# Where a retention-and-FFN kernel places its small side work: copies of turned q and k, and the preparation of w_out

## The chip, the cores and the metric

The kernel runs on one core of one Trainium2 chip. The metric is the device time of that core in microseconds (us), over repeated executions. A few terms are used throughout. PE is TensorE, PEld its weight loads, DVE is VectorE, ACT is ScalarE, POOL is GpSimd. PSUM holds PE's products; SBUF holds the other tiles on the chip. One execution of a kernel is profiled, and the span of the trace is about 1.7 us shorter than the time measured for that execution.

## The reference

```python
def _attn_ref(q, k, v):                       # q, k, v: 8 batches, 8 heads, 576 tokens, 64 wide
    scores = scale * np.matmul(q, k.transpose(0, 1, 3, 2))
    gamma = 1.0 - 2.0 ** (-5.0 - np.arange(H, dtype=np.float32))
    ...
    Dmat = np.where(rel >= 0, gamma[:, None, None] ** rel[None, :, :], 0.0)
    return np.matmul(scores * Dmat[None], v)

def _moe_ref(x, w_in, w_out):                 # x: 4608 x 512, w_in: 512 x 2048, w_out: 2048 x 512
    h = np.maximum(x @ w_in, 0.0)
    return (h * h @ w_out).astype(np.float32)

# reference: x = attention output, batch by batch, heads side by side; result = _moe_ref(x, ...)
```

Retention (attention without softmax, with a decay per head) makes the 4608 rows of x; a feed-forward layer with squared ReLU follows. Its two weight matrices are fed to the core as 64-bit numbers, and w_out has to be turned into 32-bit numbers on the core by bit operations before it can be used.

## The kernel before

The attention goes through the tokens in chunks of 128. Between the parts of a chunk's attention, the kernel runs **steps** of the first FFN product: a block is 512 tokens, and block n is done in 28 steps (n, mp, j), with mp from 0 to 3 and j from 0 to 6. The seven values of j are the seven products of a Strassen-like scheme, each four matmul calls in the code. Both matrices' sums for that scheme are done by DVE. The second FFN product, with w_out, begins only after the last attention chunk and the steps then left, at 583.5 us.

One chunk runs like this:

```python
            retain_a(i - 1)
            ...
            move(C, i)            # copies of turned q and k that chunk i needs now
            ffn(i - 1, 0)         # steps, "first half"
            retain_b(i - 1)       # q'U (turned q times the state U of earlier chunks), then a tiny ACT copy of two PSUM columns
            if i < N_CH:
                scores(i)
            retain_c(i - 1)       # the rest of the chunk; ACT copies x out of PSUM
            if N_TURN <= i + 2 < N_CH:
                flip(i + 2)       # queues two DVE transposes and 16 ACT copies
            ffn(i - 1, 1)         # steps, "second half"
```

The tiny copy matters because the matmuls of `retain_c` wait for it, and ACT takes its work in the order of issue.

```python
    def retain_b(i):
        ...                       # q'U on PE
        nc.scalar.copy(u_sb[(2 * ci + (cs // CH)) % 3][:, 0:2, 0:1], xp[0][:, :, cs - CH:cs - CH + 1])

    def retain_c(i):
        ...
        while at < tok + cs:
            n = at // TOK
            while steps and steps[0][0] <= n - 2:
                step()            # steps left over at a block's end
            end = min(tok + cs, (n + 1) * TOK)
            nc.scalar.copy(xT[n][...], p[...])        # frees the single x_ps tile
```

After its product, each step empties the product's PSUM buffer on ACT or DVE. A later product takes that buffer, so PE may have to wait for it:

```python
        elif j == 3:
            nc.scalar.activation(g["A11"], p, AF.Relu)                                # ACT, L638
            nc.gpsimd.tensor_tensor(g["A11"], g["A11"], g["A11"], op=ALU.mult)        # POOL, L639
        elif j == 4:
            nc.vector.tensor_tensor(g["A22"], p, p15, op=ALU.add)                     # DVE, L641
            square(g["A22"])                                                          # DVE, L629
```

Then each step may carry one **part** of the preparation of w_out, 139 parts in all. A piece of w_out is five DVE instructions and one pair on ACT; the outer sums follow after every second piece:

```python
    def w_out_parts():
        ...
            for one, two, beside, *_ in pair:
                yield one                 # DVE L210
                yield two, beside         # DVE L214, ACT L218 and L219: the conversion pair
            for i, (_, _, _, three, four, five) in zip((j - 1, j), pair):
                yield three               # DVE L222
                yield four                # DVE L225
                yield last                # DVE L228, and the fetch of a later piece
            ...
                r1, r2, r3, r4 = right_sums(*b)                # DVE L245 to L248
                yield lambda r1=r1, r2=r2: (r1(), r2())
                yield lambda r3=r3, r4=r4: (r3(), r4())
        ...
    # at the end of a step:
        if n_w2[0] < 0.9 * (done[0] - N_0):                                  # pace
            if not (busy[0] or held[0] and type(w_out_next[0]) is tuple):    # a tuple is L214 with its pair
                ...                                                          # issue the next part
```

## Time and profile before

| | before |
|---|---|
| time, median of 3 runs (range) | 985.23 us (984.21 to 985.42) |
| span of the trace | 981.6 us |
| PE busy, whole span | 954.2 us, 97% |
| first product of w_in in the steady part to last matmul of attention | 421.7 us |
| from there to the first product with w_out | 55.3 us |
| products with w_out | 398.1 us |

The three lower rows are read from the start times of PE's instructions. The change touches only the first of them. Two groups of instructions of the page before give the two engines that PE can be held up by there (line, engine, operation, tiles, shapes and count; then busy us and mean ns of one; then idle time before them and what ended most of it):

```profile
L622 PE MATMUL h_b<-room,w 128*128 128x256 f32 x768 | 186.6, 386 | 6.7 <-DVE room L641 3.7
L411 ACT COPY qk<-flip 32x256 f32<-32x256 f32 x416 | 167.4, 402 | 16.4 <-DVE flip L396 10.7
```

PE's products of one of three kinds lose 6.7 us to waits, 3.7 of them for L641. ACT's copies of turned q and k are 167.4 us of work in small instructions of 0.4 us: whatever comes after them in ACT's order has to sit through them. The waits themselves, and what lies ahead of them, are shown in the prediction.

### The profile page before, as it was taken

Reading aid. Unit: us, or ns where it says so; the run is one execution under the profiler, and the core shown is the slowest. Engines: PE = TensorE matmul, PEld = TensorE weight load, DVE = VectorE, ACT = ScalarE, POOL = GpSimd, SP = SyncE. Lnnn points to the kernel's source line nnn. Section 1 sums busy time; section 2 is a strip of 40 time slices with the busy share of each in tenths; the row PEclk is TensorE's granted clock in tenths of the full one; section 3 lists DMA queues with packets and bytes.
Section 4 is the critical chain, followed back from the end, with each engine's and each line's share of the span. In section 5 each row is a group of like instructions: output and inputs, shape, how many; then the busy total and the mean of one; then the engine's idle time right before and its main releaser. Section 6 shows DMA issues by size and latency. Waiting matters only on the chain. (4 is left out here: it accounts for less than half of the span.)

```text
span 981.6 us, 24018 instructions
## 1 busy us (share of the span) xinstructions
PE 954.2 (97%) x10108; PEld 850.8 (87%) x10108; DVE 781.8 (80%) x1447; ACT 341.6 (35%) x848; POOL 128.1 (13%) x121
## 2 busy tenths in 40 slices
PE   7799999999999989989999999999999999999998
PEld 6645787888878878878888889999999999999998
DVE  4789798978887988788756588878888787887876
ACT  3454384674755855846541010000000000000000
POOL 3221223312122221213201000000000000000000
PEclk9999999999999999999999999999999999999999
DMA  9975656785586767655636967645353454634241
GB/s 201 241 222 152 180 149 168 210 271 152 146 247 197 202 177 232 172 146 134 240 131 237 360 246 251 226 161 184 108 204 115 177 186 170 209 114 172 87 172 43
DMA packets 172011, 181.43 MB, mean 185 GB/s; under 512 B 118144, under 2 KB 132480, under 8 KB 165248
## 3 DMA queue, kind: packets, MB, share of 16 engines
q1 hardware_dynamic: 169792, 179.38, 57.9%
q8 instruction: 79, 1.29, 0.5%
q10 hardware_dynamic: 2112, 0.52, 0.2%
q14 instruction: 28, 0.23, 0.1%
HBM read 109.36 MB, written 70.52 MB: 183 GB/s over the span
## 5 line engine op out<-in xcount | busy, mean ns | idle before, releaser
L622 PE MATMUL h_b<-room,w 128*128 128x256 f32 x768 | 186.6, 386 | 6.7 <-DVE room L641 3.7
L411 ACT COPY qk<-flip 32x256 f32<-32x256 f32 x416 | 167.4, 402 | 16.4 <-DVE flip L396 10.7
L622 PEld LDWEIGHTS h_b<-room,w 128*128 128x128 f32 x768 | 144.0, 191 | 29.0 <-DVE room L641 4.9
L928 PE MATMUL o_b<-w,room 128*128 128x128 f32 x1168 | 144.4, 275 | 0.2 <-DVE room L880 0.2
L928 PEld LDWEIGHTS o_b<-w,room 128*128 128x128 f32 x1168 | 137.2, 192 | 0.4 <-DVE room L880 0.4
L928 PE MATMUL o_c<-w,room 128*128 128x128 f32 x1008 | 123.0, 275 | 0.0
L622 PE MATMUL h_a<-room,w 128*128 128x256 f32 x512 | 122.5, 382 | 0.0
L622 PE MATMUL h_c<-room,w 128*128 128x256 f32 x512 | 122.1, 381 | 0.0
L928 PEld LDWEIGHTS o_c<-w,room 128*128 128x128 f32 x1008 | 117.7, 192 | 0.0
L942 ACT COPY r<-o_a 128x128 f32<-128x128 f32 x53 | 14.1, 266 | 271.6 <-PE o_a L928 236.0
L622 PEld LDWEIGHTS h_a<-room,w 128*128 128x128 f32 x512 | 96.0, 190 | 13.9 <-issue 0.5
L622 PEld LDWEIGHTS h_c<-room,w 128*128 128x128 f32 x512 | 96.4, 190 | 13.4
L928 PE MATMUL o_a<-w,a 128*128 128x128 f32 x688 | 85.6, 275 | 0.0
L928 PEld LDWEIGHTS o_a<-w,a 128*128 128x128 f32 x688 | 81.2, 192 | 0.1
L639 POOL TENSOR_TENSOR room<-room 128x512 f32<-128x512 f32 x32 | 34.8, 1086 | 346.3 <-ACT room L638 291.8
L629 DVE SCALAR_TENSOR_TENSOR room<-room 128x512 f32<-128x512 f32 x96 | 71.5, 745 | 3.3
L586 PE MATMUL h_ps<-room,w 128*128 128x512 f32 (+1 forms) x152 | 58.9, 535 | 2.7 <-DVE w L228 1.8
L641 DVE TENSOR_TENSOR room<-h_b,room 128x512 f32<-128x512 f32 x32 | 22.0, 687 | 45.5 <-PE h_b L622 45.5
L376 POOL TENSOR_TENSOR q_ld<-q_ld,dv 128x512 f32<-128x512 f32 (+1 forms) x39 | 45.8, 1175 | 90.3 <-DMA q_ld<-in_q_dram 56.0
L465 PEld LDWEIGHTS x_ps<-qk,v_ld 64*64 64x64 f32 x1152 | 40.3, 136 | 19.4 <-issue 12.1
L465 PE MATMUL x_ps<-qk,v_ld 64*64 64x64 f32 x1152 | 49.6, 226 | 6.4 <-ACT u_sb L503 6.0
L453 POOL TENSOR_TENSOR v_ld<-v_ld,dv 128x512 f32<-128x512 f32 (+1 forms) x40 | 48.6, 1215 | 15.0 <-DMA v_ld<-in_v_dram 7.6
(104 smaller groups left out, 1339.8 us busy)
## 6 DMA issues: line engine op xcount, KB each, us to landing
g_dram<-room SPq DMA_DIRECT2D x32, 1280.0 KB, 5.7
a<-g_dram SPq DMA_DIRECT2D x30, 1024.0 KB, 6.1
room<-g_dram SPq DMA_DIRECT2D x15, 1024.0 KB, 5.6
w<-w_dram SPq DMA_DIRECT2D x7, 1792.0 KB, 9.8
out_dram<-room SPq DMA_DIRECT2D x17, 512.0 KB, 3.3
w<-in_moe_w_in_dram SPq DMA_DIRECT2D x16, 512.0 KB, 5.9
w<-in_moe_w_out_dram SPq DMA_DIRECT2D x16, 512.0 KB, 3.9
v_ld<-in_v_dram SPq DMA_DIRECT2D x31, 256.0 KB, 3.8
```

The costliest lines, as they stand in the source:

```text
L376: engine.tensor_tensor(t, t, dv[:cs, :, NCH + ci:NCH + ci + 1].to_broadcast([cs, H, D]), op=ALU.mult)
L411: nc.scalar.copy(*moves.pop(0)[2:])
L453: nc.gpsimd.tensor_tensor(vs[:cs], vs[:cs], dv[:cs, :, ci:ci + 1].to_broadcast([cs, H, D]), op=ALU.mult)
L465: own.append(lambda hp=hp, e=e, b=b: nc.tensor.matmul(x_at(hp, b, h), lhsT=s["vs"][rows(h), 2 * hp + b, :], rhs=s["ret"][rows(h), e, hp, : ...
L586: nc.tensor.matmul(p.rearrange("p h t -> p (h t)"), lhsT=w[:, c, :], rhs=xT[0][:, c, lo * HT:hi * HT], start=(c == 0), stop=(c == N_DM - 1))
L622: nc.tensor.matmul(p[:, mm, :], lhsT=w[:, c, :], rhs=xs[n][right][:, c, :], start=(j in OPENS and mm == 0 and c == 0), stop=(j in CLOSES a ...
L629: nc.vector.scalar_tensor_tensor(t, t, 0.0, t, op0=ALU.max, op1=ALU.mult)
L639: nc.gpsimd.tensor_tensor(g["A11"], g["A11"], g["A11"], op=ALU.mult)
L641: nc.vector.tensor_tensor(g["A22"], p, p15, op=ALU.add)
L928: nc.tensor.matmul(p, lhsT=s["lefts"][left][:, m, :], rhs=w_out[j][:, m, WO_SLOT[right], :], start=(i in OPENS and m == 0), stop=(i in CLO ...
L942: nc.scalar.copy(r[:, 0, 0:128], p)
```

## The change

Its intent is to keep three things out of the way of PE. Copies of turned q and k go two to a step, not three or four, in the half in front of q'U, and as before none in its last step, so that ACT is free when the tiny copy comes. No part of w_out goes into a step that carries a transpose, and no conversion pair into the last two steps of the first half. The outer sums of w_out go one to a step (155 parts in place of 139); to keep pace, steps j = 0 and 3 may take two parts, and the pace goes from 0.9 to 0.92 parts a step.

```diff
                 r1, r2, r3, r4 = right_sums(*b)
-                yield lambda r1=r1, r2=r2: (r1(), r2())
-                yield lambda r3=r3, r4=r4: (r3(), r4())
+                yield from (r1, r2, r3, r4)
@@ end of a step
-        if n_w2[0] < 0.9 * (done[0] - N_0):
-            if not (busy[0] or held[0] and type(w_out_next[0]) is tuple):
+        late_w2 = 0.92 * (done[0] - N_0) - n_w2[0]
+        for _ in range(0 if busy[0] else 2 if late_w2 > 1.5 and j in (0, 3) else late_w2 > 0):
+            if not (held[0] and type(w_out_next[0]) is tuple):
                 n_w2[0] += 1
                 f = w_out_next[0]
                 w_out_next[0] = next(w_out_steps, None)
                 for f in f if type(f) is tuple else (f,):
                     f and f()
-            if n == N_BLK - 2 and (mp, j) in ((2, 3), (3, 3)):
-                assert w_out_next[0] is None
-                fetch_w2(mp - 2)
+        if n == N_BLK - 2 and mp == 3 and j in (0, 3):
+            assert w_out_next[0] is None
+            fetch_w2(j // 3)
@@ in ffn
         while steps and count:
-            held[0] = half == 0 and count == 1
-            if not held[0]:
-                move(4 if len(moves) > 8 else 3)
-            busy[0] = len(flips) > 1
+            held[0] = half == 0 and count <= 2
+
+            move(4 if half and len(moves) > 8 else 3 if half else 2 if count > 1 else 0)
+            busy[0] = len(flips) > 0
```

## The prediction

> **What bounds the kernel now.** I read the page first, then busy time by stretch, then the waits of TensorE (PE) between 100 and 600 us, then ScalarE's (ACT) and VectorE's (DVE) instructions in order of time ahead of each wait, last the weight loads.
>
> Busy time in three stretches: the start; the stretch that the change touches; the w_out products. Columns: length, busy us (and count) of PE, PEld, DVE, ACT, POOL, then clock, DMA share, GB/s.
>
> ```profile
> 0.00:106.00 106.00, 94.84 (x1475) 61.36 (x1476) 79.29 (x131) 45.92 (x95) 26.10 (x31) 1.00 0.75 195
> 106.00:590.00 484.00, 471.29 (x5160) 401.54 (x5159) 388.21 (x610) 263.23 (x631) 102.02 (x90) 1.00 0.66 202
> 590.00:981.60 391.60, 388.10 (x3476) 387.91 (x3474) 314.31 (x708) 32.47 (x122) 0.00 (x0) 1.00 0.45 161
> ```
>
> PE is the bound throughout. Where the change works it stands idle 484.0 - 471.3 = 12.7 us. That is the whole purse, apart from slow clock and small gaps hidden in the modelled ends. The waits that make it up (total us, times, longest):
>
> ```profile
> PE x_ps L465 <- ACT u_sb L503: 5.5, 5, 1.5
> PE h_b L622 <- DVE room L641: 3.7, 3, 2.0
> PE h_b L622 <- DVE room L549: 2.2, 1, 2.2
> PE h_b L622 <- DVE room L634: 0.7, 2, 0.5
> ```
>
> Five times PE waits, after q'U and the scores, for a tiny ACT copy (0.16 us) that stands behind other ACT work; six times a product waits for DVE. Two examples. ACT ahead of a wait that ends at 253.78:
>
> ```profile
> 250.13 0.72 ACT L218 ACTIVATE w<-w,exp_bias 128x512 uint32<-128x512 uint32 x1
> 250.76 0.67 ACT L219 ACTIVATE w<-w 128x512 f32<-128x512 uint32 x1
> 251.46 1.65 ACT L411 COPY qk<-flip 32x256 f32<-32x256 f32 x4
> 253.13 0.60 ACT L638 ACTIVATE room<-h_a 128x512 f32<-128x512 f32 x1
> 253.62 0.16 ACT L503 COPY u_sb<-x_ps 128x2 f32<-128x2 f32 x1
> ```
>
> No line has idle time in front: ACT is simply late by two conversions of w_out and four copies. DVE ahead of the longest L641 wait, with POOL in the same time:
>
> ```profile
> 424.36 0.40 DVE L245 TENSOR_TENSOR w<-w 128x256 f32<-128x256 f32 x1
> 424.80 1.15 DVE L246 TENSOR_TENSOR w<-w 128x256 f32<-128x256 f32 x1
> 425.87 1.27 DVE L247 TENSOR_TENSOR w<-w,w 128x256 f32<-128x256 f32 x1
> 427.18 1.16 DVE L248 TENSOR_TENSOR w<-w,w 128x256 f32<-128x256 f32 x1
> 428.26 0.68 DVE L641 TENSOR_TENSOR room<-h_b,room 128x512 f32<-128x512 f32 x1
> ...
> 424.63 1.04 POOL L639 TENSOR_TENSOR room<-room 128x512 f32<-128x512 f32 x1 [10.59 <-ACT room L638]
> 425.63 1.24 POOL L376 TENSOR_TENSOR q_ld<-q_ld,dv 128x512 f32<-128x512 f32 x1
> 426.83 1.24 POOL L453 TENSOR_TENSOR v_ld<-v_ld,dv 128x512 f32<-128x512 f32 x1
> ```
>
> All four outer sums of w_out fall in two steps, in the 3.4 us in which POOL does its three products, and three of them take 1.2 us in place of 0.4. The clock after that wait:
>
> ```profile
> 423.30:429.00 5.70, 3.71 (x17) 2.95 (x17) 5.59 (x8) 3.49 (x9) 3.44 (x3) 1.00 1.09 298
> 429.00:432.60 3.60, 3.60 (x12) 2.41 (x12) 2.63 (x5) 1.28 (x2) 0.00 (x0) 0.53 0.42 83
> ```
>
> For 3.6 us the clock is 0.53, so the wait costs about 1.7 us more than its length.
>
> **What the Trainium skill says.** "TensorE: Matmul & The Clock Gate", section "What's actually happening": the clock is halved after an idle activity window of about 3.4 us, and the windows run freely. The trace agrees (0.53 over 3.6 us), though a 2.2 us wait at 293.8 did not halve it. The same page, "Architectural detail", has ACT and DVE as strict FIFO and PE as reordering weight loads only; both examples show it. "SBUF — State Buffer", section "Who interferes with whom": a DVE instruction with two SBUF inputs contends with a GpSimd one that reads SBUF. The four sums above show 0.40 us free, 1.15 to 1.27 us beside POOL. "Perfetto Trace Analysis", section "Identifying the Most-Contended Engine", warns that matmul busy time is no measure of nearness to roofline; so I count gaps in the stream, not busy share.
>
> **The change part by part.** It removes no work: PE's and POOL's instruction order is identical, DVE has the same instructions in another order, ACT too (but for how runs of copies fold). Only places move.
> (1) In the half in front of q'U, copies of turned q and k go two to a step rather than three or four, and none in the last step (as before).
> (2) In the last two steps there, not the last one, no conversion pair (L218 and L219, 0.72 + 0.67 = 1.4 us of ACT).
> (3) A step with either transpose gets no w_out part; before, the second one's step did.
> (4) Outer sums one to a step: 155 parts in place of 139. To keep pace, two parts go into steps j = 0 and 3 when they are behind. The last part falls late in block 7, near 523 us, not at its first steps; the first reload of w_out goes four steps later, but is needed only at 589 us, some 60 us on.
>
> I followed each wait into the new order. "Worth" is its length in PE's stream against the usual spacing, which exceeds the idle time shown where weight loads wait too.
> - 127.96 (1.3): ACT had 8 copies, a pair, 4 copies ahead. Now 8 and 2: 1.4 + 0.8 = 2.2 us less. Gone, -1.3.
> - 159.50 (1.65): a pair was held up by DVE right in front of the copy. The pair moves away. -1.65.
> - 253.92 (1.65): about 15 copies and two pairs become 10 copies and one pair. The ReLU of j = 3 still stands in front, so a little may stay. -1.5.
> - 347.04 (1.2): a pair and two copies less, 2.2 us. -1.2.
> - 527.53 (0.4): nothing queued ahead. Unchanged.
> - 151.49 (0.4): L228, 1.55 us beside POOL, leaves. -0.4.
> - 237.42 and 423.29 (0.35 and 0.6): DVE comes from the burst at a block's start (x's sums, two transposes); w_out work there is equal to 0.3 us. Unchanged.
> - 293.79 (2.3, behind x's sum L549): one sum of 0.55 us leaves; the part beside POOL (1.41) is replaced by another. -0.5.
> - 367.63 (1.7): L228 and one of four outer sums leave, but three still lie beside POOL. -0.8.
> - 429.00 (2.15 plus 1.7 of clock): L228 and four sums (4.6 us) become two wider sums, 1.2 to 2.8 us. L641 then ends by 427, in time. -3.85.
> Sum: -1.3 - 1.65 - 1.5 - 1.2 - 0.4 - 0.5 - 0.8 - 3.85 = -11.2 us.
>
> What it adds: in chunk 14 (64 rows, one step in its first half, near 187 us) two pairs now fall in the two steps ahead of that one. ACT then has a ReLU, a pair, four copies, a pair in front of the copy: 0.6 + 1.4 + 1.65 + 1.4, the second pair behind DVE's L641 and L629. I estimate 0.8 us of new wait. For other new ones I allow 0.8 us: DVE is busy 388 of 484 us, and doubled parts at j = 3 run into POOL's three products, which start when the ReLU of j = 3 ends. Net -11.2 + 1.6 = -9.6 us: 985.2 - 9.6 = 975.6 us.
>
> **The rivals.** (a) The waits only move. For: DVE's work is the same, and two parts at j = 3 sit at the worst place for POOL. Against: the waits come where DVE is late from a block's first step, and the change thins just those; the w_out work spreads over 12% more parts and steps. This gives 980 to 986. (b) All waits but the last go, and nothing new comes: -15 us, 970. Against: the bursts at 237, 293 and 423 are hardly touched. (c) Copies held back pile up, and scores wait for turned q and k: up to 8 are forced out in front of a first half (before, 8 at most too, but less often 8). That is 3.3 us of ACT against three steps of 1.73 us; I expect no wait. (d) DMA sets the end: stage buffers are written out and refilled, with six steps (10 us) between in the tightest place against transfers of about 10 us. If one is late, DVE blocks, and a stall of 2 us or more comes with slow clock: 978 to 982.
>
> **Range and chances.** The purse is 12.7 us of idle time, about 1.7 of slow clock, and 1 to 2 of small gaps: at most 16 us, 1.6%. Faster by over 2% would need 19.7 us, more than there is. Slower by over 2% would need many new waits in a kernel whose PE order does not change. So within 2% is nearly sure: 0.975, with 0.01 faster and 0.015 slower. The range is from (b) short of its best, 971, to a half-failed change, 981.5.
>
> **What would show it right or wrong.** PE idle from 106 to about 580 us falls from 12.7 to 3 to 5 us; waits on u_sb L503 fall from 5.5 to about 1.5, one of them new near 185 us; waits on L641 from 3.7 to about 1; the one on L549 stays above 1; L634's stay; no slow clock near 420 us; the stretches before 106 and after the last attention step keep their lengths. It is wrong if L641 waits come back at j = 3 doublings beside POOL, if DVE's L214 or L210 waits for a DMA, or if ACT's copies reach the scores late (a wait of sc_ps on L411).

## The result, and the profile after

| | before | after |
|---|---|---|
| time, median of 4 runs each, same rounds | 984.72 us (982.80 to 985.42) | 975.11 us (973.27 to 976.20) |
| ratio | | 0.9901, 95% interval 0.9882 to 0.9921 |
| span of the trace | 981.6 us | 974.5 us |
| w_in products and attention, as above | 421.7 us | 413.4 us |
| from there to the first product with w_out | 55.3 us | 55.3 us |
| products with w_out | 398.1 us | 398.7 us |

Ratios and intervals are from runs of the same rounds; a ratio is not quite that of the two medians (0.9902 here). The time fell by 9.6 us, within 2%. All of it lies in the stage that the change touches (8.2 us in the profiled pair); the stages after it kept their lengths to 0.6 us.

Busy time by stretch in the kernel after, in the columns of the prediction's first fence; the middle stretch is cut 7 us sooner, since the span is 7.1 us shorter:

```profile
0.00:106.00 106.00, 94.35 (x1474) 61.51 (x1475) 78.14 (x130) 46.00 (x95) 26.82 (x31) 0.95 0.76 195
106.00:583.00 477.00, 471.36 (x5168) 402.88 (x5167) 386.56 (x614) 263.42 (x631) 102.04 (x90) 1.00 0.67 206
583.00:974.50 391.50, 387.92 (x3470) 387.34 (x3468) 313.76 (x706) 32.34 (x122) 0.00 (x0) 1.00 0.45 160
```

PE's idle time in the stretch went from 12.7 us to 477.0 - 471.4 = 5.6 us. What PE waits for between 100 and 600 us in the kernel after (line numbers are one lower than before: L640 was L641, L502 was L503, L548 was L549):

```profile
PE x_ps L464 <- issue: 2.0, 2, 1.2
PE h_b L621 <- DVE room L548: 1.9, 1, 1.9
PE x_ps L464 <- ACT u_sb L502: 1.5, 3, 0.9
PE o_b L928 <- DVE room L880: 0.2, 1, 0.2
```

The waits for L641 and L634 are gone, and the waits for the tiny copy fell from 5.5 to 1.5 us. A row that was not there before has come: 2.0 us put down to "issue", which says only that the profile shows nothing that PE waited for.

The wait at 253.78 in the kernel before was ACT's lateness by two conversion pairs and the copies around them. The same place in the kernel after, on ACT in order of time:

```profile
246.28 0.68 ACT L219 ACTIVATE w<-w 128x512 f32<-128x512 uint32 x1
246.98 2.48 ACT L410 COPY qk<-flip 32x256 f32<-32x256 f32 x6
249.78 0.60 ACT L637 ACTIVATE room<-h_a 128x512 f32<-128x512 f32 x1 [0.31 <-issue]
250.27 0.16 ACT L502 COPY u_sb<-x_ps 128x2 f32<-128x2 f32 x1
```

The last pair is now ahead of six copies rather than in the last two steps, and ACT even has 0.31 us of idle time in front of the ReLU: it has caught up. The wait is gone.

The longest L641 wait ended at 428.94. The same place in the kernel after, first DVE, then POOL:

```profile
418.36 0.66 DVE L247 TENSOR_TENSOR w<-w 128x512 f32<-128x512 f32 x1
419.06 0.69 DVE L248 TENSOR_TENSOR w<-w 128x512 f32<-128x512 f32 x1
420.27 0.69 DVE L640 TENSOR_TENSOR room<-h_b,room 128x512 f32<-128x512 f32 x1 [0.52 <-PE h_b L621]
421.00 1.22 DVE L628 SCALAR_TENSOR_TENSOR room<-room 128x512 f32<-128x512 f32 x1
...
419.22 1.43 POOL L638 TENSOR_TENSOR room<-room 128x512 f32<-128x512 f32 x1 [10.92 <-ACT room L637]
420.61 1.05 POOL L375 TENSOR_TENSOR q_ld<-q_ld,dv 128x512 f32<-128x512 f32 x1
```

DVE now does two sums of w_out where it did four, one of them before POOL starts. L640 has 0.52 us of idle time before it, ended by PE: DVE waits for the product, not the product for DVE.

PE's instructions are the same in both kernels and come in the same order, so the start of each can be compared between the two traces. Where the difference of the starts jumps, a wait was won or lost. This **ledger** of jumps, in us, is the main instrument from here on. Places are times in the kernel before.

| place | what PE waited for | predicted | measured |
|---|---|---|---|
| 119.91 | POOL v_ld | nothing said | -0.36 |
| 127.96 | tiny copy | -1.3 | -1.24 |
| 151.49 | DVE, beside L228 | -0.4 | -0.37 |
| 159.50 | tiny copy | -1.65 | -1.65 |
| 182.77, chunk 14 | tiny copy, new | +0.8 | +1.03 |
| 231.16 | "issue", new | in an allowance of +0.8 | +0.88 |
| 237.42 and 423.29 | L634 | 0 | -0.35 and -0.62 |
| 253.92 | tiny copy | -1.5 | -1.47 |
| 293.79 | L549 (x's sum) | -0.5 | -0.31 |
| 291 | slow clock, new | 0 | +1.64 |
| 347.04 | tiny copy | -1.2 | -0.84 |
| 367.63 | L641 | -0.8 | -1.50 |
| 429.00 | L641 | -2.15 | -2.15 |
| 431 | slow clock | -1.7 | -1.74 |
| 479.12 | "issue", new | in the allowance | +1.22 |

These sum to -7.8 us; with jumps of under 0.15 us each it is -8.24 us between 119 and 500 us. The start (+0.51) and the end (+0.63) make the -7.1 us by which the spans of the two profiled executions differ. The medians differ by 2.5 us more; the section on the clock comes back to that.

The wait at 182.77 was predicted ("near 187"). ACT in the kernel after, ahead of it:

```profile
176.11 0.72 ACT L218 ACTIVATE w<-w,exp_bias 128x512 uint32<-128x512 uint32 x1
...
177.42 1.66 ACT L410 COPY qk<-flip 32x256 f32<-32x256 f32 x4
179.10 0.72 ACT L218 ACTIVATE w<-w,exp_bias 128x512 uint32<-128x512 uint32 x1
179.73 0.67 ACT L219 ACTIVATE w<-w 128x512 f32<-128x512 uint32 x1
180.29 0.15 ACT L502 COPY u_sb<-x_ps 128x2 f32<-128x2 f32 x1
```

A pair, four copies, a pair, without a gap, and then the tiny copy: the case that the prediction worked out for the short chunk, whose first half has a single step.

The two new "issue" waits were not predicted by place. In the kernel after, ACT and then PE around the longer of them:

```profile
469.76 0.72 ACT L218 ACTIVATE w<-w,exp_bias 128x512 uint32<-128x512 uint32 x1 [5.93 <-DVE w L210]
470.39 0.66 ACT L219 ACTIVATE w<-w 128x512 f32<-128x512 uint32 x1
470.95 0.35 ACT L521 COPY room<-x_ps 128x256 f32<-128x256 f32 x1
...
471.40 0.27 PE L464 MATMUL x_ps<-qk,v_ld 64*64 64x64 f32 x2 [1.16 <-issue]
```

ACT had been idle for 5.93 us; the pair itself waited for DVE's L210. Behind the pair in ACT's order stands L521, the copy that empties the only x_ps tile. PE's next attention product starts 0.1 us after that copy's end. So the wait named "issue" looks like a wait for the tile, and the cause a conversion pair that was put into one of the leftover steps inside `retain_c`, right in front of the copy. Whether that is so is tested below.

### The profile page after: what moved, and what is told of

The parts are those of the page before. It is cut to its first block, busy times and chain, and to the rows that moved or that the text cites. A ratio compares the mean times of both kernels' runs of the same rounds, so it can differ in the third digit from the quotient of the medians.

```text
span 974.5 us, 24019 instructions
## 1 busy us (share of the span) xinstructions
PE 953.6 (98%) x10108; PEld 851.7 (87%) x10108; DVE 778.5 (80%) x1447; ACT 341.8 (35%) x848; POOL 128.9 (13%) x121
## 4 chain that ended last, share of the span: by engine, by line
PE 92%; DVE 3%; ACT 2%; DMA 2%; issue 1%; SPq 0%; DVEq 0%
PE h_b L621 17%; PE o_b L928 17%; PE h_a L621 11%; PE h_c L621 11%; PE o_a L928 11%; PE o_c L928 11%; PE h_ps L585 4%; PE x_ps L464 3%; PE x_ps L499 2%; PE sc_ps L442 2%; DMA g<-g_dram 1%; PE u_ps L467 1%; DVE w L225 1%; DVE w L228 1%; PE t_ps L421 0%
## 5 line engine op out<-in xcount | busy, mean ns | idle before, releaser
L621 PE MATMUL h_b<-room,w 128*128 128x256 f32 x768 | 185.7, 385 | 1.9 <-DVE room L548 1.9
L621 PEld LDWEIGHTS h_b<-room,w 128*128 128x128 f32 x768 | 143.8, 190 | 22.9 <-issue 2.0
L621 PE MATMUL h_c<-room,w 128*128 128x256 f32 x512 | 122.8, 383 | 0.0
L621 PE MATMUL h_a<-room,w 128*128 128x256 f32 x512 | 122.5, 382 | 0.0
L621 PEld LDWEIGHTS h_c<-room,w 128*128 128x128 f32 x512 | 97.0, 191 | 13.7
L621 PEld LDWEIGHTS h_a<-room,w 128*128 128x128 f32 x512 | 96.0, 190 | 13.9 <-issue 0.5
L628 DVE SCALAR_TENSOR_TENSOR room<-room 128x512 f32<-128x512 f32 x96 | 73.7, 767 | 3.3
L640 DVE TENSOR_TENSOR room<-h_b,room 128x512 f32<-128x512 f32 x32 | 22.1, 690 | 49.5 <-PE h_b L621 49.5
```

Of the source, the lines that this page charges most:

```text
L621: nc.tensor.matmul(p[:, mm, :], lhsT=w[:, c, :], rhs=xs[n][right][:, c, :], start=(j in OPENS and mm == 0 and c == 0), stop=(j in CLOSES a ...
L628: nc.vector.scalar_tensor_tensor(t, t, 0.0, t, op0=ALU.max, op1=ALU.mult)
```

## The experiments

Two theories about the gain as a whole were to be told apart. **Theory A:** it comes from where parts of w_out happen to fall. A handful of places are bad (a pair ahead of the tiny copy; DVE work of two SBUF inputs ahead of L641 while POOL is at its products), the kernel before hit some of them, and any shift that misses them gains as much; the rules of the change are only one way to shift. **Theory B:** it comes from the rules, each of which removes its own kind of wait, so the parts of the change add up, and shifts without a rule gain nothing. Beside these stood the smaller questions of what the copies' rule is worth, whether the "issue" wait is what it seems, and what makes the clock slow.

Kernels of one group below ran on one chip and share the runs of the kernel before. All gave the right result.

### First group: the parts of the change, one at a time

The median of the kernel before was 984.04 us in this group (11 runs).

**The copies' rule alone,** on the kernel before:

```diff
-            if not held[0]:
-                move(4 if len(moves) > 8 else 3)
+            move(4 if half and len(moves) > 8 else 3 if half else 2 if count > 1 else 0)
```

> The kernel before with the copies' rule of the change alone (two to a step in front of q'U, none in its last step; conversions, transposes and outer sums as before). My theory, that each wait is ACT or DVE late by a countable queue: ACT has two copies (0.82 us) less ahead of the tiny copy in three of the five waits, so 127.96 falls from 1.24 to about 0.4, 253.92 from 1.47 to about 0.65, 347.04 from 0.84 to about 0; 159.50 (1.65, a conversion pair that waits for DVE) stays, and so do all waits for DVE. About -2.5 us against before. Rival, copies are the change and the rest is trimming: -7 us or more.

Measured: 983.55 us, ratio 0.9987 (0.9966 to 1.0007), so -0.5 us by the medians where -2.5 was expected, and not told apart from nothing. The ledger has -0.82, -0.92 and -0.81 at 127.96, 253.92 and 347.04, which are the three places worked out for it. So the rule's own part was right, and its side effects were missed: four new waits of 0.24 to 0.43 us came, one of them an attention product that waits for DVE's mask product of the scores (0.4 us), and the profile has a second slow clock, at 295 us. Copies taken out of the first half are done elsewhere, and there they delay others.

**The outer sums one to a step alone** (155 parts; the reloads of w_out as in the kernel after):

```diff
-                yield lambda r1=r1, r2=r2: (r1(), r2())
-                yield lambda r3=r3, r4=r4: (r3(), r4())
+                yield from (r1, r2, r3, r4)
```

> The kernel before with the outer sums one to a step alone (155 parts; old copies, old holds, old pace). My theory: it shifts where every part falls. The longest L641 wait (2.15 us) goes, with its slow clock unless another wait takes it; the ACT waits at 159.50, 253.92 and 347.04 go because the pairs fall elsewhere, 127.96 (1.24) stays; but pairs now fall between the last matmul of a chunk and the copy that frees its PSUM tile (at two block ends), two pairs each: about 2.2 us new wait in each. Net -2 to -5 us. Rival, the sums were the burden on DVE and splitting them is the gain: -7 us or more.

Measured: 976.72 us, ratio 0.9927 (0.9907 to 0.9946), so -7.3 us by the medians: more than expected. The ledger shows why. Beside the L641 waits (-1.70 at 367.63, -2.15 at 429.00 and the clock behind it), it has -1.65, -1.47 and -1.19 at 159.50, 253.92 and 347.04, which are waits for the tiny copy on ACT. A rule for sums on DVE cured waits on ACT, because 16 more parts shift every later part, and so the pairs. So the total is what the rival named (-7 us or more), but 4.3 us of it are waits on ACT, and the shifts below cure the waits for DVE without any split. The new waits at the two block ends came with 1.22 us each, not 2.2.

**The holds and the pace alone** (sums still two to a part, copies as before):

```diff
@@ end of a step: as in the change, with late_w2 and two parts at j = 0 and 3
@@ in ffn
-            held[0] = half == 0 and count == 1
-            if not held[0]:
+            if not (half == 0 and count == 1):
                 move(4 if len(moves) > 8 else 3)
-            busy[0] = len(flips) > 1
+            held[0] = half == 0 and count <= 2
+            busy[0] = len(flips) > 0
```

> The kernel before with the holds and the pace alone (no pair in the last two steps before q'U, no part beside either transpose, two parts at j = 0 and 3 when late; outer sums in pairs, copies as before). My theory: the four ACT waits of chunks 10, 12, 19 and 26 nearly go (-5), the L641 waits go (-3.5 to -5 with the clock), new waits of about 2 us where two pairs stand in front of the chunk's copy from PSUM near 230 us and of about 1.5 us at chunk 34 with a pair directly in front of the tiny copy. Net -6 to -8 us, the largest of the three parts alone. Rival, any reordering moves the waits without removing them: within 2 us of before.

Measured: 977.64 us, ratio 0.9936 (0.9918 to 0.9955), so -6.4 us, as expected. The ledger has the same -1.65, -1.47, -1.19, -1.70 and -2.15, and five new waits of its own, of 0.57 to 2.29 us. Their places were partly missed: near 230 us 1.22 came and not 2, at chunk 34 (458 us) nothing, and the longest, at 266.71, was not foreseen. It had been expected to be the largest of the three parts; the split gained more, with overlapping intervals.

**The whole change without the copies' rule:**

```diff
-            move(4 if half and len(moves) > 8 else 3 if half else 2 if count > 1 else 0)
+            if not (half == 0 and count == 1):
+                move(4 if len(moves) > 8 else 3)
```

> The changed kernel with the copies' rule of before (three or four to a step). My theory: copies matter little once the pairs are away: 0.5 to 2 us slower than the changed kernel (8 copies for 6 ahead of chunk 19, 9 for 6 with a pair at chunk 26). Rival, copies are the change: 4 us slower or more.

Measured: 975.55 us, ratio 0.9911 (0.9894 to 0.9929). The whole change has 0.9901 and, measured again below, 0.9888; by these the copies' rule is worth 1 to 2.3 thousandths, some 1 to 2 us, and the intervals overlap.

What follows from the group: the three parts alone give -0.5, -7.3 and -6.4 us by the medians, 14 us together, and the whole gives 9.6. They do not add, because two quite different rules cured the same waits at the same places. That speaks against B.

### Second group: a shift without a rule, and the waits that remain

The median of the kernel before was 982.92 us in this group (11 runs).

**The kernel before, with all parts of w_out about three steps later and no rule changed:**

```diff
-        if n_w2[0] < 0.9 * (done[0] - N_0):
+        if n_w2[0] < 0.9 * (done[0] - N_0) - 3:
```

> The kernel before with none of the change's rules: w_out's parts only start three parts later (0.9 times the steps, less 3), so the same rule meets other steps. Theory A, the gain is where the parts happen to fall: ahead of the tiny copies of chunks 10 and 12 there is no pair now (-2.9), at 367.6 and 429 two or three short parts stand in the place of the sums (-1.5 and -2.2 to -3.8), one pair stands in front of a chunk's copy from PSUM near 230 us (+0.9): -6 to -8 us. Theory B, the rules themselves (holds, split, two copies) carry the gain: within 2 us of before.

Measured: 975.61 us, ratio 0.9918 (0.9902 to 0.9934). A change of one constant gives eight of the ten thousandths. The ledger has most of the same entries: -1.18, -1.65, -1.12 and -1.91 at 127.96, 159.50, 367.63 and 429.00; the wait at 253.92 stays, as expected. Theory A's total and these four places held. Its new wait near 230 us did not come; 0.73, 0.90 and 0.67 us came at 142.67, 172.49 and 414.33, and 347.04 went too (-1.19).

**The whole change, with three conversion pairs issued later:** in the leftover steps of `retain_c` a pair is put off until the copy of x_ps has been issued, and the second pair ahead of chunk 14's tiny copy until that one has.

```diff
@@ retain_b, after the tiny copy
+        catch_up()
@@ retain_c
+            put_off[0] = True
             while steps and steps[0][0] <= n - 2:
                 step()
+            put_off[0] = False
             ...                                    # the copies of x_ps
+        catch_up()
@@ end of a step
-                    f and f()
+                    if f and f.__name__ == "beside" and put_off[0]:
+                        later.append(f)            # catch_up() issues what is in this list
+                    else:
+                        f and f()
@@ in ffn
+            put_off[0] = put_off[0] or i == 13 and half == 1 and count == 1
```

> The changed kernel with three conversion pairs issued on ACT later: those of the two block ends (near 230 and 471 us) behind the chunk's copy from PSUM, that of chunk 14 (near 181 us) behind its tiny copy. DVE's order is the same. If the three new waits of the changed kernel (0.88, 1.22, 1.11 us) are these pairs, all three go, -3 us against the changed kernel in the stream of products. Rival, the wait for the chunk's tile is for another thing (POOL's product of v): they stay and the time is within 0.5 us of it.

Measured: 970.95 us, ratio 0.9874 (0.9855 to 0.9893). Against the kernel after, the ledger has -1.03, -0.88 and -1.22 us at just the three places, -3.13 in all; about +0.5 comes back at 478, just behind the last of them, and nothing else on the way moved by more than the clock's own steps. So the wait named "issue" was a wait for the copy that frees the x_ps tile, and its cause the pair in front of that copy: this is shown, since the two traces differ in ACT's order at just three places (each time the copy now stands ahead of the pair), and DVE's order is identical. The wait for x's sum stays.

**The whole change, with two DVE instructions taken from in front of x's second sum** in block 3 (a part of w_out at one step, and a sum of g one step later):

```diff
-        if j in (6, 0, 1, 2, 3):
+        if j in (6, 0, 1, 2, 3) and (n, mp, j) != (3, 3, 6):
@@ end of a step
-        for _ in range(0 if busy[0] else 2 if late_w2 > 1.5 and j in (0, 3) else late_w2 > 0):
+        for _ in range(0 if busy[0] or (n, mp, j) == (3, 3, 4) else 2 if ... else late_w2 > 0):
```

> The changed kernel with DVE relieved ahead of its largest wait (1.98 us near 290 us): no w_out part in the last step before block 4 (1.5 us beside POOL), and one sum of g taken behind x's sums (0.6 us). Theory: DVE is late by the sum of its queue, the wait falls to 0 to 0.5 us and the slow clock behind it (1.5 us in the profiled run) goes too: -2 to -3 us against the changed kernel. Rival, DVE waits there for PE and the queue does not matter: unchanged.

Measured: 971.92 us, ratio 0.9876 (0.9857 to 0.9894). The wait for L548 fell from 1.9 to 0.6 us (-1.27 in the ledger), and its profile has no slow clock near 291. A few later parts of w_out fell a step later as well, until the count had caught up; no other wait in the ledger moved.

**Both:**

> Both repairs in one: the pairs later and block 4 relieved. If the waits are independent, -4.5 to -6 us against the changed kernel, 969 to 971 us, and PE idle between the first product with w_in and the last attention step under 2 us. Rival, they move on: less than 2 us.

Measured: 968.96 us (968.00 to 973.22), ratio 0.9855 (0.9834 to 0.9876): 14.5 thousandths below the kernel before, and some 3 to 5 below the kernel after. The second comparison goes through the kernel before, since the kernel after did not run in this group; the interval lies below the first one of the kernel after (from 0.9882) and just touches the second (from 0.9871). What PE still waits for between 100 and 600 us (the edit moves lines: L625, L552 are L621, L548):

```profile
PE h_b L625 <- DVE room L552: 0.6, 1, 0.6
PE x_ps L464 <- ACT u_sb L502: 0.5, 2, 0.4
PE o_b L943 <- DVE room L895: 0.2, 1, 0.2
```

From 106 to 570 us PE is busy 462.7 of 464.0 us. The purse of the stage is spent.

### Third group: more neutral shifts, one wait by itself, and the change once more

The median of the kernel before was 985.60 us in this group (11 runs). A neutral shift is one that changes no rule.

**The kernel before, with five and with eight empty parts ahead of w_out's first:**

```diff
     def w_out_parts():
+        yield from [None] * 5          # or 8
```

> The kernel before with none of the change's rules, but five empty parts ahead of w_out's: every part falls elsewhere among the steps. Theory A (place, not rule): no pair stands ahead of the tiny copies of chunks 10, 12, 19 and 26 (-5), short parts instead of four sums ahead of both L641 waits (-3 to -5 with the clock), two pairs in front of a chunk's copy from PSUM near 230 us (+1.2), other new ones 1: -6 to -9 us. Theory B (the kernel before is at an ordinary place and starting three parts later was a lucky one): within 3 us of before.

> The same with eight empty parts, a third place. Theory A: the pairs ahead of chunks 10, 12 and 26 go, the sums leave block 5's and 6's fourth steps, one pair comes directly in front of chunk 34's tiny copy (+1.2) and two sums into the burst at block 5's start (+0.5): -5 to -9 us. Theory B: within 3 us of before.

Measured: five give 977.69 us, ratio 0.9927 (0.9907 to 0.9947); eight give 974.48 us, ratio 0.9887 (0.9870 to 0.9904). With eight, the ledger has -9.83 us between 119 and 500 us. That is the whole gain of the change, with none of its rules. (Shifts are not all alike: the largest new waits of five are 1.89, 1.21 and 1.16 us at 142.67, 231.16 and 332.86; those of eight are 1.15, 0.78 and 0.56 us at 332.86, 490.28 and 240.33. The total of five was expected; eight gained 11.1 us by the medians, more than the 5 to 9 expected, and the wait expected at chunk 34, at 458 us, did not come.)

**The kernel before, with no part of w_out in two steps ahead of the longest wait:**

```diff
-        if n_w2[0] < 0.9 * (done[0] - N_0):
+        if n_w2[0] < 0.9 * (done[0] - N_0) and (n, mp, j) not in ((6, 0, 2), (6, 0, 3)):
```

> The kernel before with two steps of block 6 (j = 2 and 3) left without a w_out part, so that the four outer sums come after the product they were in front of; nothing else. Theory: the longest L641 wait (2.15 us) goes and does not come back later; the slow clock behind it goes too unless another wait of about 2 us earlier takes it: -2 us (-3.8 with the clock) in the stream of products. Rival, DVE's work is the bound of this stretch and the wait moves on: 0.

Measured: 981.54 us (977.63 to 986.39), ratio 0.9968 (0.9943 to 0.9992). The ledger has -2.15 us at 429.00 and -1.74 us of clock behind it, and no wait elsewhere in exchange. These two make -3.9 us; the sum of the stage is only -2.3, because this profile has a slow clock at 294 us that the profile of the kernel before did not have. The wait there is the same in both; the next part takes that up. The runs' times scatter by 9 us, more than those of any other kernel here.

**The change itself, again:**

> The changed kernel itself, beside the shifted ones on the same chip: 0.990 of before, as on record. Its profile shows whether slow clock follows the 2 us wait near 290 us again: if the activity windows run freely, it may be absent or of the same 3.4 us, worth 0 or 1.6 us.

Measured: 974.29 us (973.78 to 974.78), ratio 0.9888 (0.9871 to 0.9905). The wait for L548 is there with its 1.9 us, and no slow clock follows it.

### The ledger of all runs, and the clock

Jumps in us against the kernel before, at the places that count; the two of L634, 119.91, 151.49 and 332.86 are left out for width. "Sum" is everything between 119 and 500 us, the clock and what was left out with it.

| kernel | 127.96 | 142.67 | 159.50 | 182.77 | 231.16 | 253.92 | 266.71 | 293.79 | 347.04 | 367.63 | 429.00 | 479.12 | sum | ratio |
|---|---|---|---|---|---|---|---|---|---|---|---|---|---|---|
| after | -1.24 | 0 | -1.65 | +1.03 | +0.88 | -1.47 | 0 | -0.31 | -0.84 | -1.50 | -2.15 | +1.22 | -8.24 | 0.9901 |
| after, again | -1.24 | 0 | -1.65 | +1.04 | +0.88 | -1.47 | 0 | -0.31 | -0.85 | -1.50 | -2.15 | +1.22 | -9.92 | 0.9888 |
| copies alone | -0.82 | 0 | 0 | 0 | 0 | -0.92 | 0 | 0 | -0.81 | 0 | 0 | 0 | +0.48 | 0.9987 |
| split alone | 0 | 0 | -1.65 | 0 | +1.22 | -1.47 | +0.67 | -0.27 | -1.19 | -1.70 | -2.15 | +1.22 | -6.59 | 0.9927 |
| holds alone | -1.17 | +0.86 | -1.65 | 0 | +1.22 | -1.47 | +2.29 | -0.07 | -1.19 | -1.70 | -2.15 | 0 | -3.79 | 0.9936 |
| no copies' rule | -1.17 | +0.89 | -1.65 | +0.82 | +0.88 | -1.33 | 0 | -0.52 | 0 | -1.50 | -2.15 | +1.21 | -8.15 | 0.9911 |
| three later | -1.18 | +0.73 | -1.65 | 0 | 0 | -0.07 | 0 | -0.34 | -1.19 | -1.12 | -1.91 | 0 | -6.94 | 0.9918 |
| five empty | -1.18 | +1.89 | -1.65 | 0 | +1.21 | -1.47 | +0.77 | +0.26 | -1.19 | -1.70 | -2.15 | 0 | -6.77 | 0.9927 |
| eight empty | -1.18 | 0 | -1.65 | +0.18 | 0 | -1.34 | 0 | +0.37 | -1.19 | -1.70 | -2.15 | 0 | -9.83 | 0.9887 |
| one wait | 0 | 0 | 0 | 0 | 0 | 0 | 0 | 0 | 0 | 0 | -2.15 | 0 | -2.26 | 0.9968 |
| pairs later | -1.25 | 0 | -1.65 | 0 | 0 | -1.47 | 0 | -0.31 | -0.84 | -1.50 | -2.15 | 0 | -10.85 | 0.9874 |
| block 3 | -1.25 | 0 | -1.65 | +1.04 | +0.89 | -1.47 | 0 | -1.58 | -0.82 | -1.50 | -2.15 | +1.21 | -11.19 | 0.9876 |
| both | -1.25 | 0 | -1.65 | 0 | 0 | -1.47 | 0 | -1.58 | -0.84 | -1.50 | -2.15 | 0 | -13.83 | 0.9855 |

A wait that is cured is cured to the same hundredths, whatever cured it: 159.50 and 429.00 hold the same -1.65 and -2.15 in nearly every row. The wait is then gone as a whole, and it can give no more than its length: so two rules that cure it do not add.

The clock needs its own look. In each profile the recorded clock changes only on a grid of 3.41 us. In the kernel before, a wait of 2.2 us ended at 293.8 and no slow clock followed. Two neighbouring windows of the grid there, in the columns of the prediction's first fence:

```profile
289.20:292.60 3.40, 2.37 (x41) 1.75 (x39) 3.37 (x7) 1.50 (x4) 0.00 (x0) 1.00 1.08 201
292.60:296.00 3.40, 2.21 (x10) 2.00 (x11) 3.40 (x7) 1.87 (x5) 0.00 (x0) 1.00 0.02 4
```

The wait lies across the border, about 1.1 us of idle time in each window. In the kernel after, the wait for the same sum is shorter, 1.9 us, and lies in one window:

```profile
287.50:290.90 3.40, 1.49 (x37) 1.27 (x37) 3.37 (x6) 2.57 (x6) 0.00 (x0) 1.00 0.00 0
290.90:294.30 3.40, 3.40 (x10) 2.65 (x9) 2.86 (x6) 0.00 (x0) 0.00 (x0) 0.50 0.21 29
```

PE is idle for 1.9 of the 3.4 us of the first, and in the second the clock is 0.50. The second profile of the same kernel has the wait across a border again and no slow clock. Over the 14 profiles (before, after and the twelve runs), from 100 us on, all 9 windows with 1.88 us or more of idle time on PE were followed by one window at half clock, and none of the 32 windows with 0.9 to 1.81 us was. So whether a wait of about 2 us costs another 1.7 us is a matter of where it falls on the grid, and differs from one execution to the next of the same kernel. This is part of the spread of single profiles: the profiled execution of the change (976.2 us) has the slow clock, and its second one (974.8 us) has not. The profiled execution of the kernel before (983.34 us) lies 1.4 us below its median, and that of the change 1.1 us above its own; these two make the 2.5 us between the profiled pair and the medians.

## Why the prediction was right

The time of 975.6 us was predicted and 975.11 measured, inside the range of 971.0 to 981.5. Taken by its own steps:

- **The bound and the purse.** Right: nothing but PE's idle time in the stage could be won. The idle time fell to 5.6 us, against 3 to 5 predicted, and the kernel with both mends, which leaves about 1.3 us of it, is 14.3 us faster than the kernel before (0.0145 x 983 us), near the 16 us called the most there is.
- **The waits for the tiny copy.** Predicted -1.3, -1.65, -1.5, -1.2; measured -1.24, -1.65, -1.47, -0.84. The count of ACT's instructions ahead of the copy carried, but for 347.04, where "a pair and two copies less" is the step that failed. The pair did not leave: in the kernel after, L218 and L219 still stand ahead of this tiny copy (at 341.23 and 341.86), with two copies behind them in place of four. The -0.84 is what two copies are worth (0.82 us). The copies' rule alone has -0.81 there, and the change without it 0.
- **The waits for DVE.** 429.00 with its clock, -3.85 predicted, -3.89 measured. 367.63 was undersized, -0.8 against -1.50: an L228 of 0.66 and an L248 of 0.42 us left, as said, but L245, which had taken 0.82 us beside POOL, now took 0.40 just ahead of it. That makes 1.5 us. 237.42 and 423.29 were taken as unchanged and went, for -0.97. Here the step that failed is "w_out work there is equal to 0.3 us". At 423.29 an L228 beside POOL had taken 1.54 us, and an L248 of 0.41 us stood in its place; at 237.42 an L222 and an L225 (1.36 us) gave way to an L210 and an L214 (0.84 us). The equal count hid an unequal time.
- **x's sum at 293.79.** -0.5 predicted, -0.31 measured: a part of 1.41 us beside POOL was replaced by an L225 of 1.54 us, as said, but it cost a little more.
- **What is added.** Chunk 14, +0.8 predicted, +1.03 measured, at the place and for the reason named. The allowance of +0.8 for the rest was too small: +0.88 and +1.22 came, and the place feared for it (j = 3, beside POOL) was not where they came. The prediction looked for pairs ahead of the tiny copy only. It missed the other ACT instruction that PE waits for, the copy that frees the single x_ps tile.
- **The clock.** The -1.7 us at 431 came. That none would appear elsewhere was a matter of chance, and in one of the change's two profiles one did (+1.64). Nor does a stall of 2 us always bring slow clock, as rival (d) has it: the wait of 2.2 us at 293.8 in the kernel before did not.

So the total was met partly by luck: about 1.7 us of gain more than worked out at 237, 367 and 423 stands against about 1.5 us of new waits beyond the estimate.

On the rivals: (a), the waits only move, failed as a whole, but 3.1 us of new waits at three places did come. (b), all go, was the kernel with both mends rather than this one. (c), copies piling up, did not show in the change; the copies' rule by itself did bring a wait of 0.4 us for the mask product of the scores. (d), a late stage buffer, did not show: no wait of L210 or L214 for a transfer came up.

What the prediction did not see at all is the answer of the experiments: the rules as such are not what the gain rests on. Three shifts of w_out's parts without any rule gave 7 to 11 thousandths, and eight empty parts as much as the whole change. The kernel before had an unlucky arrangement. In the change itself, the -0.84 at 347.04 does rest on a rule, that of the copies: without it the entry is 0. That a different shift would always gain is not shown; only three were run, and each brought some waits of its own.

## What to carry to other kernels

When side work is dealt out to steps by a count, a change of any rule shifts all that comes after it; so follow each wait by its place in the bound engine's stream before crediting the rule, and run a neutral shift as a control. List every instruction on the slower queues that the bound engine waits for, the one that only frees a buffer too, and keep dealt-out work behind those instructions rather than spreading it evenly. Here that meant to put off three pairs and two DVE instructions by a step or so, for a further 3 to 5 us.

## What the Trainium skill lacked or had wrong

- "TensorE: Matmul & The Clock Gate", section "What's actually happening", gives an idle window of about 3.4 us as what halves the clock. The grid of 3.41 us agrees. But the window need not be idle throughout: 1.88 us of idle time in one was enough in 9 of 9 cases, and 1.81 us was not in any of 32. The same wait of 1.9 us was followed by a half-clock window in one profile of a kernel and not in another, so it should be budgeted as a chance and not as a certainty.
- "SBUF — State Buffer", section "Who interferes with whom", has the rule and no durations for this pairing. In these runs a DVE sum of two SBUF inputs took up to 1.28 us beside POOL in place of 0.40 to 0.43 (128x256), 1.41 in place of 0.55 (128x384), and up to 1.55 in place of 0.68 (128x512); L640 and L644, with one input from PSUM, stayed at 0.64 to 0.69. POOL was at times the one that lost: its product of 1.04 us took 1.43 while L248 beside it kept to 0.69.
- No page that was read says that a wait for a PSUM tile to come free can be shown as "issue", with nothing named as its releaser. Two such waits, 0.88 and 1.22 us in the ledger, turned out to be for an ACT copy that empties the tile; issuing two ACT instructions behind that copy removed them.
